# A linear-attention and snake-MLP kernel on one core: batch 0's loads, opening and three later orders rearranged

## Chip, core and metric

The kernel runs on one core of a Trainium2 chip. The metric is the device time of one execution in microseconds; the median of three runs before the change is 284.15 us (284.1 to 284.52). Times inside the kernel are from one profiled execution and are counted from its first instruction.

## What is computed

Inputs are float32: q, k, v of shape (8 batches, 8 heads, 576 rows, 64), w_in (512 x 2048), w_out (2048 x 512) and alpha (2048).

```python
q_s = softmax(q, axis=-1)                      # over the 64 of a head
k_s = softmax(k, axis=2)                       # over the 576 rows
kv  = einsum('bhsd,bhse->bhde', k_s, v)
x   = einsum('bhsd,bhde->bhse', q_s, kv)       # -> (4608 tokens, 512)
h   = x @ w_in
s   = sin(alpha * h)
g   = h + s * s / (alpha + 1e-9)
out = g @ w_out                                # (4608, 512)
```

## The kernel before

**Tiling.** A batch's 576 rows lie as 64 groups of J = 9 rows, and two heads share the 128 partitions; `ii` (0 or 1) names a half of the eight heads. The 4,608 tokens are worked in nine tiles of MF = 512 (index `t`), and the 2,048 columns of w_in in 16 blocks of 128 (index `ni`). A slot (`h_slot`) is four matmuls over `ki` (the four parts of the 512 inputs), a sine on ScalarE, a square on ScalarE, GpSimd or VectorE, and `combine` on VectorE (L270), which writes `g`. The output matmuls (L274) sum over the 16 blocks.

**Attention of a batch.** ScalarE takes the exponent of q and k (L119). q is normalised by its row sums (reduce L151, reciprocal L152, scale L153, into `qn`), then transposed into `qT`: batches 0 and 1 on TensorE, through PSUM (L203), the later ones by a DMA transpose on SyncE (L213). v is cast to bf16 into `vb`, with a column of ones beside each head. `kv_mm` (L174) multiplies the exponent of k with `vb`; the column of ones gives the sums of k, by which `kv_norm` (L184, L187) divides into `kbd`. `attn_chunk` and `attn_out` multiply `kbd` with `qT`; the result is cast into `xT`, the input of the slots.

**Order.** The schedule is written out by hand: each engine runs its instructions in the order of the program text, and a later one doesn't overtake an earlier one. `take(os, n)` issues the next n of the 64 output matmuls of a tile as work between other steps. A DMA is issued in its engine's order (SP is SyncE's queue, POOL is GpSimd's), and an instruction that waits on SP or POOL holds what stands behind it.

**Opening, up to the first slots.** SyncE loads batch 0: q's first half, k's first half, q's second, v's first, k's second (L299, called from the loop at L302). Of q only eight of the nine groups are loaded; the ninth of batches 0 and 1 comes later as `q8` (L474). GpSimd copies one element of k's first half into `held` (L332), which makes it wait for that load; behind it GpSimd issues v's second half in two parts, w_in in six column pieces (two DMAs each, one for either 64 partitions, L109) and w_out. w_in and w_out are cast from float32 to bf16 by the DMA. `warm_up(n)` (L343) issues n matmuls whose result nobody reads. Then exponents, norms, transposes and `kv_mm` follow for either half, the attention chunks, and the first matmuls of slots 0 to 3 over `ki` 0 and 1, which need only the first half of x.

**Batch 1** is loaded while tile 0's slots run: q by halves, then k and v by halves (L420, L428). Its attention stands between the output matmuls of tile 0: 46 of them, `transpose_q1(0)`, four, `kv_mm` of the first half, `kv_norm`, four, `x_half(0)`, `transpose_q1(1)`, two, `kv_mm` of the second half, `kv_norm`, five, `x_half(1)`, the rest. `x_half` and the transposes share two PSUM banks (pool "a").

**Batch 2** has its attention between the output matmuls of tile 1: four chunks (`c` from 0 to 3) with one output matmul behind each, then a piece for the last three groups. Its DMA transpose is issued in two halves; chunks 2 and 3 need the second.

**The loop over t from 3 on** does the slots of tile t, the output matmuls of tile t - 1 (an accumulator is copied out after every 16 and stored by two DMAs on SyncE, L286 and L289), and the attention of batch t + 1. `q_transpose_dma` of that batch and the loads of the one after it are issued at `ni == 4`; the attention's first matmul that needs the transpose comes at `ni == 9`.

Of the kernel before, what the change touches and what calls it, by code (L numbers as in the profile page):

```python
# [15 lines left out]
F32 = mybir.dt.float32  # L16
# [7 lines left out]
def kernel(  # L24
# [14 lines left out]
    nc = tc.nc  # L39
# [77 lines left out]
    def exp_to(dst, src, iis=range(2)):  # L117
        for ii in iis:
            nc.scalar.activation(dst[:, :, ii * 128:(ii + 1) * 128].rearrange("p j (x d) -> p x j d", x=2),  # L119
                                 src[:, ii::2], AX.Exp)  # L120
# [2 lines left out]
        A["qe", b] = att2.tile([128, J, 4 * D], BF16, name="qe")  # L123
        exp_to(A["qe", b], staged["q", b])

    def exp_half(name, b, ii, j1=J):
        if ii == 0:
            A[name + "e", b] = att2.tile([128, J, 4 * D], BF16, name=name + "e")
        exp_to(A[name + "e", b][:, 0:j1], staged[name, b][:, :, 0:j1], (ii,))

    def exp_k(b):
        A["ke", b] = att2.tile([128, J, 4 * D], BF16, name="ke")
# [165 lines left out]
    def load0(eng, n, t, ii, j0=0, j1=J):  # L298
        eng.dma_start(out=staged[n, 0][:, ii::2, j0:j1].rearrange("p i j d -> p i (j d)"),  # L299
                      in_=src_view(t, 0)[:, ii::2, j0 * D:j1 * D])  # L300

    for n, t, ii in (("q", q, 0), ("k", k, 0), ("q", q, 1), ("v", v, 0), ("k", k, 1)):  # L302
        load0(nc.sync, n, t, ii, 0, 8 if n == "q" else J)
    nc.scalar.dma_start(out=alpha_rows, in_=moe_alpha.rearrange("(no ni) -> no ni", ni=128))
    make_identity(nc, ident)
    DVE_CP(identb, ident)
# [23 lines left out]

    held = singles.tile([128, 1], F32, name="held")
    GP_CP(held, staged["k", 0][:, 0, 0, 0:1])  # L332
    load0(GP, "v", v, 1, 0, 5)
    load0(GP, "v", v, 1, 5, 9)
    for c0, c1 in ((0, 256), (256, 512), (512, 768), (768, 1024), (1024, 1536), (1536, 2048)):
        load_win(c0, c1)
    for c in range(2):
        load_wout(4 * c, 4 * c + 4)
# [1 line left out]
    def warm_up(n):  # L340

        for _ in range(n):
            nc.tensor.matmul(warm, identb, A["qe", 0][:, 0:4, 0:128], start=True, stop=True)  # L343

    exp_half("q", 0, 0, 8)
    exp_half("k", 0, 0)
    exp_half("q", 0, 1, 8)
    warm_up(7)  # L350
    norm_q(0, [V, V], 8)
    q_tile(0)
    q_transpose_ii(0, 0, 0, 8, tp0)
# [52 lines left out]
    def take(it, n=1000):  # L406
        for _ in range(n):
            if next(it, 0) == 0:
                return
# [4 lines left out]
    with ES:  # L414
        def load_q1(ii):
            if ii == 0:
                staged["q", 1] = stage.tile([128, 4, J, D], F32, name="st_q", tag="st")
            st = staged["q", 1]
            DVE_CP(st[:, ii, 0, 0:1], zero)
            nc.sync.dma_start(out=st[:, ii::2, 0:8].rearrange("p i j d -> p i (j d)"),  # L420
                              in_=src_view(q, 1)[:, ii::2, 0:8 * D])

        def load_kv1():
            for n in "kv":
                staged[n, 1] = stage.tile([128, 4, J, D], F32, name=f"st_{n}", tag="st")
# [12 lines left out]

        accs = [bank(kind) for kind in "bbll"]
        os = o_quad(0, accs, [DVE_CP, ACT_CP, DVE_CP, DVE_CP])  # L440
        take(os, 46)
        for ii in range(2):
            exp_half("q", 1, ii, 8)
        norm_q(1, [GP, V], 8)
        GP_CP(held, staged["k", 1][:, 0, 0, 0:1])
        load_wout(14, 16)

        def cast_v1(ii, eng):
            vv = vb[1].rearrange("p j (i c) -> p i j c", i=4)
            eng(vv[:, 2 * ii:2 * ii + 2, :, 0:D], staged["v", 1][:, ii::2])  # L450

        exp_half("k", 1, 0)
        cast_v1(0, ACT_CP)
        exp_half("k", 1, 1)
        def transpose_q1(ii):
            tp = ps_h[0].tile([128, 8, 128], BF16, name="tp", tag="a")
            q_transpose_ii(1, ii, 0, 8, tp)
            DVE_CP(q_tile(1)[:, ii, 0:8], tp)

        transpose_q1(0)  # L460
        take(os, 4)

        def x_half(ii):
            xp = [bank("a") for _ in range(2)]
            for e in range(2):
                attn_chunk(1, 2 * ii + e, 0, 8, xp[e])
            for e in range(2):
                (ACT_CP, DVE_CP)[e](xT[:, 2 * ii + e, MF:2 * MF], xp[e])
# [24 lines left out]
        load("v", v, 3)  # L493

        def late_q8(ni):
            if ni == 11:
                tp = ps_k.tile([128, 2, 2, 128], BF16, name="tp", tag="a")
                for b in range(2):
                    for ii in range(2):
                        nc.tensor.transpose(tp[:, ii, b], A["qe", 1][:, J - 2 + b, ii * 128:(ii + 1) * 128], identb)  # L500
                DVE_CP(A["qT", 1][:, :, J - 2:J], tp)
            elif ni == 15:
                xp = ps_k.tile([128, 4, 2, P], F32, name="xp", tag="a")
                for c in range(4):
# [75 lines left out]
    for t in range(3, nT):  # L580
        b = t + 1 if t + 1 < B else None
        os = o_stream(t - 1)
        done = 0
        if b is not None:

            exp_q(b)
            exp_k(b)
            cast_v(b, [GP_CP, GP_CP])
            norm_q(b, [GP])
            take(os, 8)  # L590
            done = 8
        for ni in range(nN):
            hp = mm_h(t, ni)
            if b is not None:
                if ni == 4:
                    q_transpose_dma(b)
                    if b + 1 < B:
                        load_batch(b + 1)
                attn_back(b, ni - 5)
            s = sine(t, ni, hp, "A")  # L600
            combine(t, ni, hp, s)
            want = 23 + 2 * (t == 3) + 21 * ni // 8 if b is not None else 4 * (ni + 1)
            take(os, min(64, want) - done)
            done = min(64, want)
        take(os)
# [36 lines left out]
```

## Time and profile before

| what | value |
|---|---|
| median of three runs | 284.15 us |
| the profiled execution, its own time | 284.61 us |
| its span, first to last instruction | 282.8 us |
| DVE / ACT / POOL busy | 189.1 / 225.2 / 83.6 us |
| granted TensorE clock | 1.000 |
| DMA packets | 39,127, 45.80 MB |
| output matmuls, L274, into `op` | 496, 124.1 us busy |
| slot matmuls, L254, into `hp` | 512, 128.3 us busy |

Busy times of matmuls overlap, since they are pipelined, so a busy PE isn't PE at its peak. In a row of the timeline the columns are start, duration, engine, line, operation, what it writes and reads, its shape and how many were merged; in square brackets stands the idle time of that engine before it and what ended it. PE is the matrix unit, PEld its weight load, DVE VectorE, ACT ScalarE, POOL GpSimd, SPq SyncE's queue.

### The profile page before, as it was taken

The numbers are of one execution on the slowest core, as the hardware profiler recorded it, in microseconds if no ns is written. First come the engines' busy times: TensorE is split into PE (matmuls) and PEld (weight loads), VectorE is DVE, ScalarE is ACT, GpSimd is POOL, SyncE is SP. The second block draws the span as 40 slices with busy tenths as digits, with TensorE's granted clock in tenths as the row PEclk, the third lists the DMA queues.
The fourth block names the chain that finished last, engine by engine and source line by source line (L and its number), as shares of the span: only waits on it lengthen the run. The fifth ranks groups of instructions, "written<-read, shape, count | busy, mean of one in ns | idle before, by whom it ended". The sixth has DMA issues, their size and how long they took to land.

```text
span 282.8 us, 4841 instructions
## 1 busy us (share of the span) xinstructions
PE 272.3 (96%) x1857; PEld 128.0 (45%) x1857; DVE 189.1 (67%) x286; ACT 225.2 (80%) x320; POOL 83.6 (30%) x80
## 2 busy tenths in 40 slices
PE   2999999999999999999999999999999999999994
PEld 1444444444444444444544444444444444444443
DVE  3968778899977768756875677667775555555412
ACT  4889667999489998899989998999877777777400
POOL 2989411777666550035012500241000000000000
PEclk9999999999999999999999999999999999999999
DMA  6999989996599018931991099019011111111143
GB/s 256 306 195 234 300 278 320 361 352 226 125 233 387 6 37 198 386 116 35 263 398 42 14 271 404 23 24 160 2 37 37 37 39 37 37 37 43 44 103 74
DMA packets 39127, 45.80 MB, mean 162 GB/s; under 512 B 17072, under 2 KB 22464, under 8 KB 39104
## 3 DMA queue, kind: packets, MB, share of 16 engines
q1 hardware_dynamic: 33360, 40.57, 47.0%
q0 software_dynamic: 5552, 4.79, 10.1%
q8 instruction: 14, 0.23, 0.3%
q10 hardware_dynamic: 192, 0.14, 0.2%
q14 instruction: 9, 0.07, 0.1%
HBM read 36.71 MB, written 9.44 MB: 163 GB/s over the span
## 4 chain that ended last, share of the span: by engine, by line
PE 82%; DMA 6%; ACT 5%; issue 2%; DVE 2%; POOL 1%; SPq 1%
PE hp L254 35%; PE op L274 32%; PE lp L274 2%; PE hp L274 2%; PE lp L254 2%; DMA qT<-qn 2%; ACT s L260 2%; DMA win<-in_moe_w_in_dram 2%; PE xp L223 2%; DMA st_k<-in_k_dram 2%; PE kvp L174 1%; PE op L612 1%; PE op L254 1%; PE kvp L254 1%; DVE qs L151 1%
## 5 line engine op out<-in xcount | busy, mean ns | idle before, releaser
L270 DVE SCALAR_TENSOR_TENSOR g<-s,inva_sb,hp 128x512 bf16<-128x512 f32 x128 | 94.3, 746 | 58.6 <-ACT s L262 52.9
L254 PE MATMUL hp<-xT,win 128*128 128x512 bf16 x512 | 128.3, 379 | 0.7 <-DMA win<-in_moe_w_in_dram 0.7
L274 PE MATMUL op<-wout,g 128*128 128x512 bf16 x496 | 124.1, 379 | 0.0
L260 ACT ACTIVATE s<-hp,alpha_sb 128x512 f32<-128x512 f32 x128 | 86.2, 682 | 24.3 <-PE hp L254 23.9
L254 PEld LDWEIGHTS <-win 128*128 128x128 bf16 x576 | 56.0, 98 | 67.9 <-DMA win<-in_moe_w_in_dram 0.8
L274 PEld LDWEIGHTS <-g 128*128 128x128 bf16 x560 | 53.9, 98 | 61.1 <-issue 0.4
L262 ACT ACTIVATE s<-s 128x512 f32<-128x512 f32 x112 | 70.5, 630 | 3.5
L264 POOL TENSOR_TENSOR s<-s 128x512 f32<-128x512 f32 x29 | 30.3, 1061 | 21.6 <-ACT s L260 21.6
L153 POOL TENSOR_TENSOR qn<-qe,qs 128x1152 bf16<-128x1152 bf16 (+1 forms) x12 | 25.1, 2110 | 33.0 <-DVE qs L147 24.3
L286 DVE COPY o<-op 128x512 f32<-128x512 f32 (+2 forms) x33 | 22.1, 670 | 9.9 <-PE op L274 7.6
L138 POOL CAST vb<-st_v 128x1152 bf16<-128x1152 f32 x12 | 14.7, 1257 | 46.9 <-DMA st_v<-in_v_dram 32.9
L119 ACT ACTIVATE qe<-st_q 128x1152 bf16<-128x1152 f32 (+1 forms) x16 | 17.5, 1130 | 5.0 <-DMA st_q<-in_q_dram 4.8
L119 ACT ACTIVATE ke<-st_k 128x1152 bf16<-128x1152 f32 x16 | 17.9, 1151 | 1.5 <-DMA st_k<-in_k_dram 1.5
L146 DVE TENSOR_REDUCE qs<-qe 128x36 f32<-128x2304 bf16 x5 | 12.8, 2553 | 7.9 <-ACT qe L119 7.9
L226 DVE CAST xT<-xp 128x512 bf16<-128x512 f32 (+1 forms) x18 | 13.5, 751 | 0.1
L151 DVE TENSOR_REDUCE qs<-qe 128x16 f32<-128x1024 bf16 (+1 forms) x6 | 7.5, 1252 | 3.8 <-ACT qe L119 3.8
L119 ACT ACT_TABLE_LOAD x7 | 9.0, 1283 | 1.3 <-PEq L626 1.2
L274 PE MATMUL lp<-wout,g 128*128 128x512 bf16 x32 | 9.1, 380 | 0.0
L274 PE MATMUL hp<-wout,g 128*128 128x512 bf16 x32 | 8.9, 380 | 0.0
L223 PE MATMUL xp<-qT,kbd 128*128 128x256 bf16 (+1 forms) x40 | 8.2, 286 | 0.3 <-DMA qT<-qn 0.3
L174 PEld LDWEIGHTS <-ke 64*64 64x64 bf16 x576 | 5.7, 108 | 4.7 <-ACT vb L329 1.3
L187 DVE TENSOR_TENSOR kbd<-kvp,kvr 64x256 bf16<-64x256 f32 (+1 forms) x20 | 7.4, 368 | 0.5
(83 smaller groups left out, 135.6 us busy)
## 6 DMA issues: line engine op xcount, KB each, us to landing
out_dram<-o SPq DMA_DIRECT2D x70, 128.0 KB, 2.4
st_q<-in_q_dram SPq DMA_DIRECT2D x6, 1152.0 KB, 6.3
st_k<-in_k_dram SPq DMA_DIRECT2D x6, 1152.0 KB, 8.8
st_v<-in_v_dram SPq DMA_DIRECT2D x6, 1152.0 KB, 11.1
st_k<-in_k_dram SPq DMA_DIRECT2D x4, 576.0 KB, 6.7
st_q<-in_q_dram SPq DMA_DIRECT2D x4, 512.0 KB, 5.2
st_v<-in_v_dram SPq DMA_DIRECT2D x3, 576.0 KB, 7.6
wout<-in_moe_w_out_dram POOLq DMA_DIRECT2D x3, 512.0 KB, 9.6
```

The costliest lines, as they stand in the source:

```text
L119: nc.scalar.activation(dst[:, :, ii * 128:(ii + 1) * 128].rearrange("p j (x d) -> p x j d", x=2), src[:, ii::2], AX.Exp)
L138: engs[ii](vv[:, 2 * ii:2 * ii + 2, :, 0:D], staged["v", b][:, ii::2])
L153: engs[ii % len(engs)].tensor_tensor(qn[:, ii, 0:j1].rearrange("p j (x d) -> p j x d", x=2), qe[:, ii], part.unsqueeze(3).to_broadcast([12 ...
L223: nc.tensor.matmul(xp[:, e, 0:n], kt[:, e, ii], qT[:, ii, j0:j1, e * 64:(e + 1) * 64], start=True, stop=True)
L226: eng(xT[:, 2 * ii:2 * ii + 2, c0:c0 + n], xp[:, :, 0:n])
L254: nc.tensor.matmul(hp, win[:, ki, ni * 128:(ni + 1) * 128], xT[:, ki, t * MF % NX:t * MF % NX + MF], start=(ki == 0), stop=(ki == 3))
L260: nc.scalar.activation(s, hp, AX.Sin, scale=alpha_sb[:, ni:ni + 1])
L262: nc.scalar.activation(s, s, AX.Square)
L264: nc.gpsimd.tensor_tensor(s, s, s, op=ALU.mult)
L270: nc.vector.scalar_tensor_tensor(G[t][:, ni], in0=s, scalar=inva_sb[:, ni:ni + 1], in1=hp, op0=ALU.mult, op1=ALU.add)
L274: nc.tensor.matmul(acc, G[t][:, ni, j * 128:(j + 1) * 128], wout[:, ni, :], start=(ni == 0), stop=(ni == nN - 1))
L286: eng(o[:, cols], acc)
```

## The change

Five things change. (1) SyncE loads batch 0 in another order: q's first half in two parts of four groups, q's second half, k, v, k, v, the last v half in two parts; GpSimd loads no v any more. (2) w_in's first 512 columns come as two halves of rows (`ki` 0 and 1, then 2 and 3) in place of two halves of columns; the other pieces stay. (3) The opening's exponents, sums, scales and casts are cut otherwise and shared anew between ScalarE and VectorE, and TensorE's transposes of q's second half stand behind the first two attention chunks; the warm-up matmuls are 7, 2 and 2 in place of 7, 2 and 3. (4) In batch 1, two output matmuls stand ahead of `transpose_q1(1)`, not behind it; in batch 2, three follow chunk 1 in place of one. (5) In the loop over t, the DMA transpose and the next batch's loads are issued at `ni == 3` in place of 4.

```diff
-    for n, t, ii in (("q", q, 0), ("k", k, 0), ("q", q, 1), ("v", v, 0), ("k", k, 1)):
-        load0(nc.sync, n, t, ii, 0, 8 if n == "q" else J)
+    for n, t, ii, j0, j1 in (("q", q, 0, 0, 4), ("q", q, 0, 4, 8), ("q", q, 1, 0, 8), ("k", k, 0, 0, J), ("v", v, 0, 0, J),
+                             ("k", k, 1, 0, J), ("v", v, 1, 0, 5), ("v", v, 1, 5, J)):
+        load0(nc.sync, n, t, ii, j0, j1)
...
     GP_CP(held, staged["k", 0][:, 0, 0, 0:1])
-    load0(GP, "v", v, 1, 0, 5)
-    load0(GP, "v", v, 1, 5, 9)
-    for c0, c1 in ((0, 256), (256, 512), (512, 768), (768, 1024), (1024, 1536), (1536, 2048)):
+    for k0 in (0, 2):
+        load_win(0, 512, k0, k0 + 2)
+    for c0, c1 in ((512, 768), (768, 1024), (1024, 1536), (1536, 2048)):
         load_win(c0, c1)
...
+    def sum_q0(ii, j0, j1):
+        nc.vector.tensor_reduce(qs0[:, j0:j1, 2 * ii:2 * ii + 2], ...)
+    def inv_q0(ii):
+        nc.vector.reciprocal(qs0[:, 0:8, 2 * ii:2 * ii + 2], qs0[:, 0:8, 2 * ii:2 * ii + 2])
+    def scale_q0(ii, j0, j1):
+        nc.vector.tensor_tensor(qn0[:, ii, j0:j1]..., qe0[:, j0:j1, ii * 128:(ii + 1) * 128]..., qs0..., op=ALU.mult)
...
-    exp_half("q", 0, 0, 8)
+    for j0 in (0, 4):
+        exp_half("q", 0, 0, j0 + 4, j0)
+        sum_q0(0, j0, j0 + 4)
+    warm_up(7)
+    inv_q0(0)
+    scale_q0(0, 0, 8)
+    exp_half("q", 0, 1, 8)
+    sum_q0(1, 0, 8)
     exp_half("k", 0, 0)
-    exp_half("q", 0, 1, 8)
-    warm_up(7)
-    norm_q(0, [V, V], 8)
+    inv_q0(1)
     q_tile(0)
     q_transpose_ii(0, 0, 0, 8, tp0)
-    cast_v0(0, 0, 9, ACT_CP)
+    warm_up(2)
+    cast_v0(0, 0, 5, DVE_CP)
+    cast_v0(0, 5, 9, ACT_CP)
     ACT_CP(A["qT", 0][:, 0, 0:8], tp0)
     exp_half("k", 0, 1)
+    kv_mm(0, 0, ps_k, split=True)
     warm_up(2)
-    kv_mm(0, 0, ps_k, split=True)
-    warm_up(3)
+    scale_q0(1, 0, 4)
     kv_norm(0, 0, 1)
-    tp1 = ps_l.tile([128, 8, 128], BF16, name="tp", tag="l")
-    q_transpose_ii(0, 1, 0, 8, tp1)
-    cast_v0(1, 0, 5, ACT_CP)
-    cast_v0(1, 5, 9, DVE_CP)
+    scale_q0(1, 4, 8)
+    cast_v0(1, 0, 5, DVE_CP)
+    cast_v0(1, 5, 9, ACT_CP)
     xp = [bank("b") for _ in range(2)]
     for c in range(2):
         attn_chunk(0, c, 0, 8, xp[c])
+    tp1 = ps_l.tile([128, 8, 128], BF16, name="tp", tag="l")
+    q_transpose_ii(0, 1, 0, 8, tp1)
...
         x_half(0)
+        take(os, 2)
         transpose_q1(1)
-        take(os, 2)
         kv_mm(1, 1, ps_k, split=True)
...
         (ACT_CP, DVE_CP)[c % 2](xT[:, c, c0:c0 + 6 * P], xp)
-        take(os, 1)
+        take(os, 3 if c == 1 else 1)
...
-                if ni == 4:
+                if ni == 3:
                     q_transpose_dma(b)
                     if b + 1 < B:
                         load_batch(b + 1)
```

More of the change, by code (lines that the diff above doesn't have):

```diff
@@ L124, in exp_q, with exp_half @@
         exp_to(A["qe", b], staged["q", b])
-    def exp_half(name, b, ii, j1=J):
-        if ii == 0:
+    def exp_half(name, b, ii, j1=J, j0=0):
+        if (name + "e", b) not in A:
             A[name + "e", b] = att2.tile([128, J, 4 * D], BF16, name=name + "e")
-        exp_to(A[name + "e", b][:, 0:j1], staged[name, b][:, :, 0:j1], (ii,))
+        exp_to(A[name + "e", b][:, j0:j1], staged[name, b][:, :, j0:j1], (ii,))
     def exp_k(b):
@@ L343, in warm_up @@
             nc.tensor.matmul(warm, identb, A["qe", 0][:, 0:4, 0:128], start=True, stop=True)
-    exp_half("q", 0, 0, 8)
+    qe0 = A["qe", 0] = att2.tile([128, J, 4 * D], BF16, name="qe")
+    qn0 = A["qn", 0] = att1.tile([128, 2, J, 2 * D], BF16, name="qn")
+    qs0 = small.tile([128, J, 4], F32, name="qs")
+    def sum_q0(ii, j0, j1):
+        nc.vector.tensor_reduce(qs0[:, j0:j1, 2 * ii:2 * ii + 2],
+                                qe0[:, j0:j1, ii * 128:(ii + 1) * 128].rearrange("p j (x d) -> p j x d", x=2),
+                                axis=AXL.X, op=ALU.add)
+    def inv_q0(ii):
+        nc.vector.reciprocal(qs0[:, 0:8, 2 * ii:2 * ii + 2], qs0[:, 0:8, 2 * ii:2 * ii + 2])
+    def scale_q0(ii, j0, j1):
+        nc.vector.tensor_tensor(qn0[:, ii, j0:j1].rearrange("p j (x d) -> p j x d", x=2),
+                                qe0[:, j0:j1, ii * 128:(ii + 1) * 128].rearrange("p j (x d) -> p j x d", x=2),
+                                qs0[:, j0:j1, 2 * ii:2 * ii + 2].unsqueeze(3).to_broadcast([128, j1 - j0, 2, D]), op=ALU.mult)
+    for j0 in (0, 4):
[6 more added lines that the diff above has]
+    sum_q0(1, 0, 8)
     exp_half("k", 0, 0)
-    exp_half("q", 0, 1, 8)
-    warm_up(7)
-    norm_q(0, [V, V], 8)
+    inv_q0(1)
     q_tile(0)
     q_transpose_ii(0, 0, 0, 8, tp0)
-    cast_v0(0, 0, 9, ACT_CP)
+    warm_up(2)
+    cast_v0(0, 0, 5, DVE_CP)
+    cast_v0(0, 5, 9, ACT_CP)
     ACT_CP(A["qT", 0][:, 0, 0:8], tp0)
     exp_half("k", 0, 1)
+    kv_mm(0, 0, ps_k, split=True)
     warm_up(2)
-    kv_mm(0, 0, ps_k, split=True)
-    warm_up(3)
+    scale_q0(1, 0, 4)
     kv_norm(0, 0, 1)
-    tp1 = ps_l.tile([128, 8, 128], BF16, name="tp", tag="l")
-    q_transpose_ii(0, 1, 0, 8, tp1)
-    cast_v0(1, 0, 5, ACT_CP)
-    cast_v0(1, 5, 9, DVE_CP)
+    scale_q0(1, 4, 8)
+    cast_v0(1, 0, 5, DVE_CP)
+    cast_v0(1, 5, 9, ACT_CP)
     xp = [bank("b") for _ in range(2)]
```

## Prediction

> **What bounds the kernel now.** I read the page first, then the sums by stretch, then the timeline around every place where the next matmul starts later than the one before it allows. The page:
>
> ```profile
> PE 272.3 (96%) x1857; PEld 128.0 (45%) x1857; DVE 189.1 (67%) x286; ACT 225.2 (80%) x320; POOL 83.6 (30%) x80
> ```
>
> TensorE is the bound, and almost all of its idle time is at the start. Matmuls of 512 columns follow each other every 0.216 us (eight of them take 1.73 us in the chain that ended last). Held against that step, PE from 16.4 us on has only three pauses over 0.2 us, and the change has an edit at each. The opening:
>
> ```profile
> 5.99 0.19 POOL L332 COPY held<-st_k 128x1 f32<-128x1 f32 x1 [4.68 <-DMA st_k<-in_k_dram]
> 6.11 1.63 POOL L299 DMA_DIRECT2D st_v<-in_v_dram  x2
> 7.73 4.96 POOL L109 DMA_DIRECT2D win<-in_moe_w_in_dram  x8
> 13.75 1.02 PE L254 MATMUL hp<-xT,win 128*128 128x512 bf16 x4 [0.67 <-DMA win<-in_moe_w_in_dram]
> ```
>
> Here the reader sees that the first useful matmul (13.75) waits for w_in, which POOL may issue only when k's first half has landed. But an earlier start is worth something only if the data of batch 1 comes earlier too. The sums by stretch (PE, PEld, DVE, ACT, POOL busy, clock, DMA share, GB/s):
>
> ```profile
> 17.00:26.00 9.00, 9.00 (x43) 4.11 (x42) 7.42 (x12) 8.85 (x16) 7.46 (x9) 1.00 1.23 202
> 26.00:33.00 7.00, 7.00 (x35) 3.14 (x33) 6.17 (x10) 5.88 (x9) 3.59 (x4) 1.00 1.19 261
> 33.00:39.00 6.00, 6.00 (x35) 2.97 (x34) 3.41 (x6) 3.04 (x3) 2.86 (x3) 1.00 1.05 402
> 41.00:44.00 3.00, 2.54 (x52) 1.39 (x52) 2.60 (x7) 0.87 (x2) 0.00 (x0) 1.00 0.58 107
> ```
>
> The DMA share is at or above 1 until 39 us (the loads that cast count their smaller written bytes, hence 202 GB/s). So when batch 1's v lands is settled by bytes, not by when PE asks. The timeline there:
>
> ```profile
> 38.18 1.17 ACT L450 CAST vb<-st_v 128x1152 bf16<-128x1152 f32 x1 [0.88 <-DMA st_v<-in_v_dram]
> ...
> 41.48 0.77 DVE L450 CAST vb<-st_v 128x1152 bf16<-128x1152 f32 x1 [0.33 <-DMA st_v<-in_v_dram]
> 42.02 0.61 PE L203 MATMUL tp<-identb,qn 128*128 128x128 bf16 x8 [0.46 <-ACT xT L468]
> 42.28 0.69 DVE L468 CAST xT<-hp 128x512 bf16<-128x512 f32 x1
> 42.89 0.68 DVE L458 COPY qT<-tp 128x1024 bf16<-128x1024 bf16 x1
> 43.54 0.17 DVE L184 RECIPROCAL kvr<-kvp 128x2 f32<-128x2 f32 x1
> 43.74 0.59 DVE L187 TENSOR_TENSOR kbd<-kvp,kvr 64x128 bf16<-64x128 f32 x2
> ```
>
> VectorE runs from v's landing (41.46) to 44.33 without a gap, and the matmul pair of x_half(1), which reads kbd, starts at 44.50. Only 0.1 us of slack is left after a semaphore's 0.05. The two later pauses:
>
> ```profile
> 72.70 0.38 PE L274 MATMUL op<-wout,g 128*128 128x512 bf16 x1
> 73.15 0.32 PE L231 MATMUL hp<-qT,kbd 128*128 128x384 bf16 x1
> ...
> 110.31 1.03 PE L254 MATMUL hp<-xT,win 128*128 128x512 bf16 x4
> 111.63 0.39 PE L223 MATMUL xp<-qT,kbd 128*128 128x256 bf16 x2 [0.30 <-DMA qT<-qn]
> ```
>
> 73.15 - 72.70 - 0.216 is 0.23 us; 111.63 - 110.31 - 4 x 0.216 is 0.46 us.
>
> **The change, part by part.**
>
> *Opening, loads.* The bytes up to w_in's first 512 KB are the same, in another order on SP: q, q, k, v, k, v. From landings of before (issue plus time to landing: 4.51 for q, then +1.43 for k, +1.27 q, +1.42 v, +1.48 k) I get q complete at 5.8, k's first half at 7.2, v 8.65, k 10.1, and v's second half at 11.55, since 576 KB on SP took 1.42 to 1.48 and on POOL 1.54 (10.11 to 11.65). POOL's held copy moves from 5.99 to 7.25, and with it w_in's first issue from 7.73 to 7.4: it no longer stands behind v's two issues (0.90 and 0.73 us). Three SP issues more cost 0.5 us each of SP's queue, which next has work at 23.43.
>
> Runs get shorter: q's halves and v's parts have 1,024 to 1,280 bytes where the loads of before have 2,048 and 2,304. The trace has packets of 256 bytes (q8's load) at 18 ns, of 2,048 at 84 and of 2,304 at 93: a fixed 8.6 ns and 0.0366 per byte, so 46 and 55.5 for the new ones. Over 16 engines q's first half costs 512 x 46 / 16 - 256 x 84 / 16 = 0.13 us more and v's second 256 x (46 + 55.5) / 16 - 256 x 93 / 16 = 0.14: I take 0.25. From the one side it is nothing (as by the 2,048-byte row); from the other, q8's load as a whole (256 KB in about 1.8 us) in place of its packets makes the same line give 0.63. Against it, w_in's first 512 columns come in runs twice as long: a 256 KB piece landed every 0.68 us when 256 wide and every 0.64 when 512 wide (1.28 for twice the bytes), so 4 x 0.04 is 0.15 back. Net: batch 1's data 0.10 us later; bounds -0.3 (short runs free, the later narrow pieces faster too) and +0.5.
>
> *Opening, compute.* Durations from the rows: exp of 1,024 takes 1.06, reduce and scale 1.22, reciprocal 0.25, ACT cast 0.73 for 640, DVE cast 0.43 for 512. ACT: q in two of 0.6 (to 5.15), q 6.9, k 8.4, v's part 9.3, qT copy 10.3, k 11.45, v's part 12.2, xT 12.8, qT 13.8 (14.20 before). DVE: two sums 5.8, reciprocal 6.1, scale 7.35, sum 8.6, reciprocal 8.85, cast 9.4, scale 10.05, kv_norm 10.95, scale 11.6, cast 12.1, xT 12.8, kv_norm 13.65. So x's first half is ready at 12.8 and w_in's first row pair (all four output blocks) at 13.5: 13.61 less two pieces' gain. PE: four matmuls to 14.4, the attention pair to 14.85, DVE's two xT casts 14.65 to 16.05. Slot 0's last part resumes at 16.1, was 16.37: the opening gains 0.3 us. One warm-up fewer overall (12 to 11) lies in idle PE. From both sides: +0.9 if w_in is there at 12.85, -0.35 if w_in's packets start 2.4 us after issue (as w_out's did at 36.41 beside running loads) and take 30% of the engines from v.
>
> *Batch 1.* The transposes waited 0.6 us for a bank (ACT's cast, 41.39 to 41.97). Two output matmuls moved ahead of them fill 0.43. PE would reach x_half(1) at 44.50 - 0.3 - 0.43 = 43.77, but kbd comes from v's landing: 41.46 + 0.10 + 2.87 + 0.05 = 44.48. So opening and filler together pay 0.02 us, and PE waits the rest. The same cap hides an opening up to 0.35 worse.
>
> *Batch 2, c == 1.* Two more output matmuls (0.43) before the third chunk, which waits for its transpose's landing: 0.23 gained. What is late next: that chunk's casts, by 0.2; DVE is in its 2.55 us reduce until 73.7 and casts at 74.73 anyway.
>
> *ni 3 for 4, in the loop.* SP's order at t=3 is the point:
>
> ```profile
> 102.68 4.82 SPq L289 DMA_DIRECT2D out_dram<-o  x4
> 107.60 1.87 SPq L213 DMA_TRANSPOSE qT<-qn  x1
> ```
>
> Its input is ready at 103.85 (POOL's two qn end there), but the transpose stands behind the second output pair, whose DVE copy starts at 105.69. Moved past it, it issues at 103.9, lands 4 us later at 107.9, and is needed at 111.17: 0.46 gained. The output pair then waits behind the transpose and three loads until 107.5, 1.1 us later; o has four buffers and the next copy is at 113.4. For t=4 to 6 no queue order changes and PE had no wait there: nothing.
>
> Sum: 0.02 + 0.23 + 0.46 = 0.71 us. The profiled execution took 284.61 (282.8 of span and 1.8 around it), 0.46 above the median of the runs; I take the difference as the same: span 282.1, execution 283.9, median 284.15 - 0.71 = **283.4**.
>
> The chip's notes speak against the order of loads: the Trainium skill, DMA: Bandwidth & Descriptors, Queues, rings and completion order, says that each engine takes turns between queues, a packet at a time, and its Latency section puts the first byte of a POOL-issued load at about 1 us. By that w_in would share with k and v from 8.4 us. Before, v's 320 KB on POOL's queue were issued at 6.11 and landed at 10.88, 0.77 after k on SP (10.11): behind it, not beside it. By the rule the sum would be that of the slower rival.
>
> **Rivals.** (1) *The opening pays too.* If batch 1's v lands 0.6 us earlier, 0.3 + 0.43 come through: 0.73 + 0.69 = 1.42, 282.7. For it: w_in's narrow pieces are the slowest loads. Against: equal bytes, a DMA share of 1. (2) *The short runs cost more*, the 0.63 of the far side, and batch 1's v is 0.48 us late: 41.46 + 0.48 + 2.92 = 44.86 against 44.50 gives back 0.36, leaving 0.33: 283.8, no difference that can be told. For it: 202 GB/s in the stretch of narrow pieces. Against: q's and k's loads, of unlike runs, moved at one rate. I count 0.2% (0.57 us) as what a measurement of this kernel can tell. (3) *Slower: w_in takes half of the engines from k and v.* Place: 8.5 us on (issue 7.4 plus 1.1, SP's own lag at the start, 0.74 to 1.87). SP's loads have 2.7 us left, become 5.4, v's last part lands at 14.35; ACT casts it (15.0), then xT (15.6) and qT (16.6); the attention pair starts at 16.65 instead of 14.61: 2.04 lost. The filler returns 0.43, the later edits 0.69: +0.92, 285.1. It decides from a loss of 1.7 in the opening on, so from sharing before about 8.8. For it: 26 to 33 us, where a q load took 6.1 us to land beside w_out. Against: the row of v's load above. (4) *The transposes don't move*, because POOL ends later than 107: 0.46 missing, 283.9; POOL's row ends at 103.85, so I fold it into (2).
>
> **How the numbers follow.** Forecast 50%, its own range 283.1 to 283.7; (1) 13%; (2) with (4) 22%; (3) 15%. Of the forecast's half 5% lie within 0.2%: faster 0.45 + 0.13 = 0.58, same 0.27, slower 0.15. The range 282.8 to 284.2 leaves out about 8% of (1)'s side and 12% of (3)'s.
>
> **What would show it.** Right: kbd of batch 1 still released by v's landing near 41.5, x_half(1) near 44.4 with a PE pause of 0.3 to 0.6 ahead of it; no pause near 73 nor 111; SP's transpose at t=3 near 103. Wrong: v of batch 1 landing before 41 or after 42; v of batch 0 landing after 13; PE at half rate (0.427 us per matmul, as at 5.64 to 8.15 us) after 13.5, which would cost 0.21 per matmul.

## The result, and the profile after

The change made the kernel slower: a median of 286.25 us (285.49 to 288.83) beside 284.45 us for the kernel before in the same comparison, a ratio of 1.0063 with a 95% interval of 1.0047 to 1.0079. The forecast was 283.4 us, faster. The profiled execution took 286.75 us, with a span of 285.0 us (282.8 before).

The page of the changed kernel first, its busy times and the granted clock in 40 slices (7.1 us each):

```profile
PE 271.3 (95%) x1827; PEld 128.6 (45%) x1856; DVE 189.8 (67%) x289; ACT 224.9 (79%) x321; POOL 82.2 (29%) x78
...
PEclk9779999999999999999999999999999999999999
```

TensorE's work is the same, 271.3 us for 272.3, so the 2.2 us of span are waiting. The clock, 9 in every slice before, is lower in the second and third: the trouble lies in the first 20 us. The timeline there (start, duration, engine, line, in brackets the idle time and what ended it):

```profile
3.65 1.36 ACT L119 ACTIVATE qe<-st_q 128x512 bf16<-128x512 f32 x2 [1.14 <-DMA st_q<-in_q_dram]
8.55 1.06 ACT L119 ACTIVATE qe<-st_q 128x1024 bf16<-128x1024 f32 x1 [3.54 <-DMA st_q<-in_q_dram]
9.98 0.19 POOL L333 COPY held<-st_k 128x1 f32<-128x1 f32 x1 [8.68 <-DMA st_k<-in_k_dram]
10.11 7.08 POOL L109 DMA_DIRECT2D win<-in_moe_w_in_dram  x11
11.94 0.71 PE L174 MATMUL kvp<-vb,ke 64*64 64x65 bf16 x36 [3.50 <-DVE vb L330]
16.01 1.46 PE L254 MATMUL hp<-xT,win 128*128 128x512 bf16 x3
```

q's first half comes early, in two parts at 3.63 and 4.36 us, as meant. But ScalarE then waits 3.54 us for q's second half, which lands at 8.53, 4.17 us after the load before it; the working had 5.8. Everything behind it in SyncE's queue is late by as much: k 9.93, v 11.36, k 12.86, v's last part 14.58 (11.65 before, 11.55 in the working). `held`, w_in's first issue (10.11 for 7.4) and the first slot matmul (16.01; 13.75 before) follow.

The sums by stretch tell whether the engines had nothing to do or were slow. The columns are the busy times of PE, PEld, DVE, ACT and POOL, the clock, the DMA share and GB/s. The clock's 1.00 can't be relied on in these rows: in the kernel before, PE's warm-ups from 5.64 us on are 0.43 us apart, twice the step at full rate. Before:

```profile
3.00:4.50 1.50, 0.25 (x1) 0.28 (x2) 0.43 (x2) 0.00 (x0) 0.00 (x0) 1.00 1.05 407
4.50:6.00 1.50, 0.36 (x1) 0.11 (x1) 0.38 (x1) 1.10 (x2) 0.01 (x1) 1.00 1.04 406
6.00:7.50 1.50, 1.50 (x5) 0.59 (x4) 1.43 (x3) 1.39 (x2) 1.50 (x3) 1.00 1.06 415
7.50:9.00 1.50, 1.50 (x8) 0.67 (x6) 1.50 (x2) 1.14 (x2) 1.50 (x4) 1.00 1.04 410
```

and after:

```profile
3.00:4.50 1.50, 0.29 (x2) 0.21 (x3) 0.62 (x3) 0.75 (x2) 0.00 (x0) 1.00 0.99 236
4.50:6.00 1.50, 1.50 (x5) 0.47 (x4) 1.42 (x3) 0.51 (x1) 0.00 (x0) 1.00 0.88 267
6.00:7.50 1.50, 1.50 (x6) 0.47 (x5) 1.24 (x2) 0.00 (x0) 0.00 (x0) 1.00 1.02 338
7.50:9.00 1.50, 0.94 (x10) 0.44 (x8) 0.00 (x0) 0.45 (x1) 0.00 (x0) 1.00 0.95 317
```

The DMA engines are as busy (share 0.88 to 1.02) but move 236 to 338 GB/s where they moved 406 to 415. That is 720 KB less in 6 us, or 1.8 us at 410 GB/s. Single packets say the same: 41 of them took over 250 ns (up to 1,076) between 3.5 and 8.4 us, and none before; 84 ns is usual for a 2,048-byte one.

How it reaches the end is seen in batch 1 (timeline of the changed kernel):

```profile
44.16 0.75 DVE L476 CAST vb<-st_v 128x1152 bf16<-128x1152 f32 x1
45.12 0.61 PE L203 MATMUL tp<-identb,qn 128*128 128x128 bf16 x8
46.57 0.59 DVE L187 TENSOR_TENSOR kbd<-kvp,kvr 64x128 bf16<-64x128 f32 x2
47.21 0.60 PE L231 MATMUL hp<-qT,kbd 128*128 128x512 bf16 x2
```

The same matmuls, `x_half(1)`, in the kernel before:

```profile
44.50 0.59 PE L231 MATMUL hp<-qT,kbd 128*128 128x512 bf16 x2
```

Batch 1's last v lands at 44.07, 2.61 us later than before (41.46). `x_half(1)` starts 3.14 us behind it (3.04 before). From its start to the end of the span it is 285.0 - 47.21 = 237.79 us; before it was 282.8 - 44.50 = 238.30. So the later edits gave 0.51 us in these two executions, and the opening took 47.21 - 44.50 = 2.71.

Two ways lead to `x_half(1)`, and here they ended close together. The one that ended last was PE's own work: from 18.14 to 47.20 us PE is busy for 28.64 of 29.06 us, without a pause over 0.16. It came late for two reasons. Its first slot was 2.26 us late (16.01 for 13.75). And from there to `x_half(1)` it took 31.20 us, where the profiles of e13, e16 and e17 below, at full clock and as free of pauses, all took 30.37; for 1.70 us of it (16.01 to 17.71) the clock stood at half. PE was busy for 1.48 us of these, half of which, 0.7 us, is my estimate of what the clock cost there, and it waited 0.22 us for w_in. The other way is v's landing: the shortest step from v to `x_half(1)` in any profile is 2.86 us, so v would have let it start at 44.07 + 2.86 = 46.93. The two are 0.28 us apart, and both are late by the opening.

The later places look as the prediction wanted them. Batch 2's third chunk, and SyncE's queue with its cause at t = 3:

```profile
74.98 0.38 PE L274 MATMUL op<-wout,g 128*128 128x512 bf16 x1
75.20 0.33 PE L231 MATMUL hp<-qT,kbd 128*128 128x384 bf16 x1
...
102.13 4.21 POOL L153 TENSOR_TENSOR qn<-qe,qs 128x1152 bf16<-128x1152 bf16 x2 [3.33 <-issue]
105.17 1.12 SPq L289 DMA_DIRECT2D out_dram<-o  x2
106.39 2.26 SPq L213 DMA_TRANSPOSE qT<-qn  x1
112.80 1.03 PE L254 MATMUL hp<-xT,win 128*128 128x512 bf16 x4
113.66 0.38 PE L223 MATMUL xp<-qT,kbd 128*128 128x256 bf16 x2
```

75.20 - 74.98 is 0.22 us, one matmul's step, so the pause of 0.23 is gone. The transpose is issued at 106.39, as soon as POOL's two `qn` end (106.34), and the matmul that needs it starts at 113.66 = 112.80 + 4 x 0.216, without a wait.

### The profile page after: what moved, and what is told of

It is laid out like the page before. It is cut to its first block, busy times and chain, and to the rows that moved or that the text cites. A ratio compares the mean times of both kernels' runs of the same rounds, so it can differ in the third digit from the quotient of the medians.

```text
span 285.0 us, 4816 instructions
## 1 busy us (share of the span) xinstructions
PE 271.3 (95%) x1827; PEld 128.6 (45%) x1856; DVE 189.8 (67%) x289; ACT 224.9 (79%) x321; POOL 82.2 (29%) x78
## 4 chain that ended last, share of the span: by engine, by line
PE 91%; DMA 5%; issue 1%; POOL 1%; DVE 1%; SPq 0%
PE hp L254 38%; PE op L274 37%; DMA st_k<-in_k_dram 3%; PE lp L274 2%; PE lp L254 2%; PE hp L274 2%; DMA win<-in_moe_w_in_dram 2%; PE kvp L174 2%; PE xp L223 2%; PE op L638 1%; PE op L254 1%; PE kvp L254 1%; POOL win L109 1%; PE hp L231 1%; SPq L299 0%
## 5 line engine op out<-in xcount | busy, mean ns | idle before, releaser
L274 PE MATMUL op<-wout,g 128*128 128x512 bf16 x477 | 121.6, 379 | 1.4 <-issue 0.6
L119 ACT ACTIVATE qe<-st_q 128x1152 bf16<-128x1152 f32 (+2 forms) x17 | 17.7, 1075 | 8.2 <-DMA st_q<-in_q_dram 8.0
L226 DVE CAST xT<-xp 128x512 bf16<-128x512 f32 (+1 forms) x18 | 13.5, 750 | 0.0
L174 PE MATMUL kvp<-vb,ke 64*64 64x65 bf16 x576 | 7.2, 200 | 3.5 <-DVE vb L330 3.5
L109 POOL DMA_DIRECT2D win<-in_moe_w_in_dram x12 | 7.5, 641 | 0.9 <-DMA win<-in_moe_w_in_dram 0.7
```

The lines of the kernel that those rows point to most:

```text
L174: nc.tensor.matmul(kvp[64 * x:64 * x + 64, e, ii * 65:(ii + 1) * 65], ke[r, j, h * 64:(h + 1) * 64], vt[r, j, h * 65:(h + 1) * 65], start= ...
L274: nc.tensor.matmul(acc, G[t][:, ni, j * 128:(j + 1) * 128], wout[:, ni, :], start=(ni == 0), stop=(ni == nN - 1))
```

## The experiments

Four theories stood at the start. A: what costs is a load of q behind another load of q. B: the split of q's first half costs, by its runs of 1,024 bytes (B1) or because two small loads of 256 KB stand at the head of the queue (B2). C: the slow load is chance. And the later edits, or the clock, might carry part of the loss. Medians are given with that of the kernel before in the same comparison in brackets, and ratios with their 95% interval. A "landing" is the last event of a load in the trace; v(1) is the landing of batch 1's last v.

**e1: the changed kernel once more**, unchanged.

> The changed kernel once more, for a second profile. In the first, q's second half landed at 8.53 us in place of the 5.8 that I had worked out, 4.2 us after the first half, and the TensorE clock stood at one half from 10.9 to 17.7 us. Theory A (q's second half is slow because it directly follows the first half of the same tensor) and theory B (the runs of 1,024 bytes slow the queue) expect it again: landing at 8 to 9 us, time 1.5 to 2 us above before. Theory C (a chance disturbance of that one execution) expects a landing near 5.8 here, and a time that differs from run to run.

286.02 us (285.21), 1.004 [1.0005, 1.0075]. q's second half lands at 7.78, 3.34 us after the load before it, v(1) at 43.27. The size varies between executions, the slow load doesn't go away: C falls.

**e2: the kernel before with the later edits alone.**

```diff
-        transpose_q1(1)
         take(os, 2)
+        transpose_q1(1)
...
-        take(os, 1)
+        take(os, 3 if c == 1 else 1)
...
-                if ni == 4:
+                if ni == 3:
```

> The kernel before with only the three later edits: two output matmuls ahead of batch 1's second transposes, three behind batch 2's chunk 1, the loop's transposes and loads at ni 3. My sum says 0.02 + 0.23 + 0.46 = 0.7 us faster than before (283.7 if before is at 284.45). All of the loss then lies in the opening. If the later edits lose time themselves, it is not faster.

284.07 us (285.21), 0.9964 [0.9947, 0.9981]: 1.1 us gained. All of the loss is in the opening.

**e3: the changed kernel with q's first half whole.**

```diff
-    for n, t, ii, j0, j1 in (("q", q, 0, 0, 4), ("q", q, 0, 4, 8), ("q", q, 1, 0, 8), ...
+    for n, t, ii, j0, j1 in (("q", q, 0, 0, 8), ("q", q, 1, 0, 8), ...
```

> The changed kernel, but q's first half comes as one load with runs of 2,048 bytes, as before; q's second half still directly behind it. Theory B expects the slow load to vanish: q's second half lands near 5.8, and the time falls by about 2 us, to 0.5 below before. Theory A expects it to stay: landing at 8 to 9, time as the changed kernel's or 0.3 above it, because the exponent of q's first half starts later.

284.5 us (285.21), 0.9976 [0.9957, 0.9996]. Its timeline:

```profile
4.99 1.15 ACT L119 ACTIVATE qe<-st_q 128x512 bf16<-128x512 f32 x2 [2.48 <-DMA st_q<-in_q_dram]
6.32 1.06 ACT L119 ACTIVATE qe<-st_q 128x1024 bf16<-128x1024 f32 x1 [0.18 <-DMA st_q<-in_q_dram]
```

Landings 4.96 and 6.30: the second q load comes 1.34 us behind the first, though it is q behind q. A falls; the split is what costs.

**e4: k between the two halves of q**, the split kept.

```diff
-    ... ("q", q, 0, 4, 8), ("q", q, 1, 0, 8), ("k", k, 0, 0, J), ...
+    ... ("q", q, 0, 4, 8), ("k", k, 0, 0, J), ("q", q, 1, 0, 8), ...
```

> The changed kernel with the loads in the order q, q, k, q, v, k, v, v: k's first half stands between q's halves as it did before. Theory A expects the slow load to vanish: k lands near 6.0, q's second half near 7.3, the time falls by about 2 us, to 0.5 below before. Theory B expects slow packets to stay, now in k's load: k lands at 7.5 or later, the time as the changed kernel's.

288.24 us (285.21), 1.0094 [1.0067, 1.0122]. Now k is the slow one: it lands at 7.50, q behind it at 8.75. Whatever load stands third is hit.

**e5: q's first half still in two loads of 256 KB, but by heads, with runs of 2,048 bytes.**

```diff
-    ... ("q", q, 0, 0, 4), ("q", q, 0, 4, 8), ("q", q, 1, 0, 8), ...
+    for i in (0, 2):
+        nc.sync.dma_start(out=staged["q", 0][:, i:i + 1, 0:8]..., in_=src_view(q, 0)[:, i:i + 1, 0:8 * D])
+    ... ("q", q, 1, 0, 8), ...
```

> The changed kernel with q's first half still in two loads of 256 KB, but cut between heads, so that the runs keep 2,048 bytes. Theory B1 (short runs at the head of the queue slow the loads behind them) expects q's second half near 6.0 to 6.5 us and a time 0.3 to 1.0 us below before. Theory B2 (it is the number of small loads ahead, not their runs) expects the slow loads again: q's second half at 7.5 or later and 1 to 2 us above before.

285.54 us (285.05), 1.0023 [0.9995, 1.005]. Landings 3.48, 4.17 and 7.58: the third load takes 3.41 us with long runs too. B1 falls, B2 holds. Its timeline shows a side effect:

```profile
4.24 1.28 ACT L119 ACT_TABLE_LOAD   x1 [4.24 <-DMA st_q<-in_q_dram]
5.54 1.15 ACT L119 ACTIVATE qe<-st_q 128x512 bf16<-128x512 f32 x2
```

Here the exponent's table load stands behind the wait for q, not ahead of it, and the early q gains nothing.

**e6: the kernel before with nothing but that split.**

```diff
-    for n, t, ii in (("q", q, 0), ("k", k, 0), ("q", q, 1), ("v", v, 0), ("k", k, 1)):
+    load0(nc.sync, "q", q, 0, 0, 4)
+    load0(nc.sync, "q", q, 0, 4, 8)
+    for n, t, ii in (("k", k, 0), ("q", q, 1), ("v", v, 0), ("k", k, 1)):
```

> The kernel before with one edit: q's first half comes in the two group parts of the change (runs of 1,024 bytes), nothing else is touched. B1 and B2 both expect k's first half, the load behind it, at 7 to 7.5 us in place of 5.94, and the time 1 to 2 us above before, since every later load moves with it. If the loss needs the change's other parts (the new order, the shared casts, the clock), the time is that of before within 0.5 us.

288.43 us (285.05), 1.0121 [1.0083, 1.016]; k at 7.75 (5.94 before), v(1) at 43.80:

```profile
7.77 1.16 ACT L119 ACTIVATE ke<-st_k 128x1152 bf16<-128x1152 f32 x1 [0.93 <-DMA st_k<-in_k_dram]
```

One line of the change, alone, is enough to make the kernel before as slow. (Part of it is the table load again: the exponent of q starts at 5.78 instead of 4.5.)

**e7: the changed kernel with 18 warm-ups for the first `warm_up(2)`**, so that PE isn't idle from 8.4 to 11.9 us and the clock stays.

```diff
-    warm_up(2)
+    warm_up(18)
```

> The changed kernel with 18 warm-up matmuls in place of 2 behind the first transposes, which fill about 3.5 us of the 3.7 that TensorE stood idle there. If part of the loss is the clock (half rate from 10.9 to 17.7 us in the first profile), the mean granted clock comes back to 0.997 or more, and the time falls by 0.6 to 1.2 us against the changed kernel, still above before by about 0.5 to 1. If the late loads are all of it, the clock rises but the time stays within 0.3 of the changed kernel's.

285.84 us (285.05), 1.003 [1.001, 1.005]. The clock is back to 0.997 to 1.0 in all executions. By the ratios the time is 0.3 us better than e1's and 0.9 better than in the first comparison, and the intervals overlap with both. The sums by stretch, of the changed kernel and then of e7:

```profile
12.00:15.00 3.00, 3.00 (x46) 1.55 (x46) 2.68 (x7) 2.44 (x4) 3.00 (x6) 0.50 1.05 192
15.00:18.00 3.00, 2.78 (x46) 1.52 (x45) 1.32 (x4) 2.97 (x5) 2.06 (x5) 0.55 1.11 143
```

```profile
12.00:15.00 3.00, 2.62 (x48) 1.07 (x47) 1.36 (x5) 2.25 (x3) 2.92 (x6) 1.00 1.08 199
15.00:18.00 3.00, 2.54 (x51) 1.53 (x51) 2.35 (x7) 2.85 (x4) 1.65 (x3) 1.00 1.20 148
```

The half clock is real, and it slows PE, but little of the loss is its own: at full clock PE waits for the late loads instead (0.86 us in e7, up to 43.24, for the cast of batch 1's first v), and v(1) lands at 44.85. In the changed kernel's profile, with v's landing as it was, only the 0.28 us between the two ways could be won back. In its 22 executions the two at clock 1.0 took 286.65 and 286.79 us, more than the median; the five at 0.993 or less took 286.75 to 288.83, but they don't say whether the clock or late data came first.

**e8: q whole, and k's first half split instead** (256 and 320 KB, third and fourth in the queue).

```diff
-    ... ("q", q, 0, 0, 4), ("q", q, 0, 4, 8), ("q", q, 1, 0, 8), ("k", k, 0, 0, J), ...
+    ... ("q", q, 0, 0, 8), ("q", q, 1, 0, 8), ("k", k, 0, 0, 4), ("k", k, 0, 4, J), ...
```

> The changed kernel with q's first half whole (2,048-byte runs), but k's first half in two parts of four and five groups (runs of 1,024 and 1,280 bytes). B1 in the form that only the head of the queue matters expects v's first half near 9.1 us and a time as with whole q, 0.5 below before. Theory B3 (short runs anywhere in the opening slow what follows) expects v's first half at 10.5 or later, and a time 1 us or more above whole q.

285.02 us (285.05), 1.0002 [0.9971, 1.0033]. Landings 4.96, 6.29, 6.96, 8.03, 9.47: no slow load. Small loads later in the queue do no harm.

**e9: the changed kernel with the second small load issued on ScalarE's queue.**

```diff
-    ... ("q", q, 0, 0, 4), ("q", q, 0, 4, 8), ("q", q, 1, 0, 8), ...
+    ... ("q", q, 0, 0, 4), ("q", q, 1, 0, 8), ...
+    load0(nc.scalar, "q", q, 0, 4, 8)
```

> The changed kernel, but the second of q's two small loads is issued on ScalarE's queue at the same time as the first on SyncE's, so that q's second half is SyncE's second load and issued 0.5 us earlier. If the slow load is slow because the engines reach the third load of one queue sooner after its issue (1.8 us) than in the kernel before (3.6 us), the earlier issue brings q's second half to 6.5 us or before and the time to within 0.5 us of before. If two small loads at the head are enough, whatever queue they stand on, it lands at 7.5 or later again and the time is 1 us or more above before.

284.96 us (285.11), 0.9998 [0.9978, 1.0018]. Its timeline and its sums by stretch:

```profile
4.22 1.15 ACT L119 ACTIVATE qe<-st_q 128x512 bf16<-128x512 f32 x2 [1.14 <-DMA st_q<-in_q_dram]
5.87 1.06 ACT L119 ACTIVATE qe<-st_q 128x1024 bf16<-128x1024 f32 x1 [0.51 <-DMA st_q<-in_q_dram]
```

```profile
3.00:4.50 1.50, 0.00 (x0) 0.00 (x0) 0.00 (x0) 0.36 (x2) 0.00 (x0) 1.00 1.10 390
4.50:6.00 1.50, 0.63 (x2) 0.31 (x3) 0.58 (x3) 0.99 (x3) 0.00 (x0) 1.00 1.05 410
```

The same bytes in the same small pieces, and 390 to 410 GB/s: q complete at 5.85, k 7.25, v 8.69, k 10.17, v 11.71. So the load behind two small ones is not slow when one of them is on another queue. e9 doesn't part the queue from the time of issue, the other reading that its expectation names: q's second half was also issued 0.5 us earlier (1.26 for 1.77 us). By the first packets, the slow loads of the change, e1, e4, e6 and e7 began 1.7 to 1.9 us after their issue and e9's 2.6 us after it. In e10, next, a load that began 1.4 us after issue was fast (k) and one that began 2.8 us after it was slow (q's second half), which speaks against that reading without settling it. (v(1) was still 42.88 here: two w_in pieces landed 2.4 us apart, at 14.41 and 16.78, which the runs below don't all show.)

**e10: one small load, k, the other small one, then q's second half.**

```diff
-    ... ("q", q, 0, 0, 4), ("q", q, 0, 4, 8), ("q", q, 1, 0, 8), ("k", k, 0, 0, J), ...
+    ... ("q", q, 0, 0, 4), ("k", k, 0, 0, J), ("q", q, 0, 4, 8), ("q", q, 1, 0, 8), ...
```

> The changed kernel with one small load at the head: q (4 groups), k's first half, q (4 groups), q's second half, v, k, v, v. If any load behind a small first one is slow, k lands at 6 us or later in place of about 5.1, and the time is 1 to 2 us above before. If it takes two small ones at the head, k lands near 5.1, q's parts at 5.8 and 7.2, and the time is 0.5 below before or up to 0.5 above it (q's first half is complete 1.4 us later).

290.54 us (285.11), 1.0201 [1.018, 1.0222], the slowest of all. k at 5.17 and the second small load at 5.83 come at nearly the usual rate (k 1.50 us behind the load ahead): one small load at the head does next to no harm. Much of the loss is another mechanism, rival (3)'s:

```profile
5.22 0.19 POOL L333 COPY held<-st_k 128x1 f32<-128x1 f32 x1 [3.91 <-DMA st_k<-in_k_dram]
5.34 5.04 POOL L109 DMA_DIRECT2D win<-in_moe_w_in_dram  x8
8.07 1.06 ACT L119 ACTIVATE qe<-st_q 128x1024 bf16<-128x1024 f32 x1 [1.59 <-DMA st_q<-in_q_dram]
13.19 1.16 ACT L119 ACTIVATE ke<-st_k 128x1152 bf16<-128x1152 f32 x1 [1.59 <-DMA st_k<-in_k_dram]
```

`held` waits for k, so w_in is issued from 5.34 and moves beside batch 0's loads: k's second half lands at 13.17, v's last part at 17.06, v(1) at 48.83. q's second half, at 8.05, was slow too (2.2 us). That wasn't w_in's doing: the first packet of GpSimd's queue ran at 9.37 us. So the load behind the second small one was slow here as well, by some 0.9 us, with k between the two.

**e11: e2 with w_in's first pieces by row halves.**

```diff
-    for c0, c1 in ((0, 256), (256, 512), (512, 768), (768, 1024), (1024, 1536), (1536, 2048)):
+    for k0 in (0, 2):
+        load_win(0, 512, k0, k0 + 2)
+    for c0, c1 in ((512, 768), (768, 1024), (1024, 1536), (1536, 2048)):
```

> The kernel before with the three later edits and w_in's first 512 columns by row halves; loads and opening as before. My price for the row halves was 4 x 0.04 = 0.15 us less load time: 0.1 to 0.3 faster than the later edits alone (0.9964 of before). If the row halves cost something (the first slots wait for other rows), it is 0.2 or more slower than these.

284.42 us (285.11), 0.9989 [0.9958, 1.002]; v(1) at 43.25. No gain over e2 (0.9964) is to be seen.

**e12: e2 with w_out's last piece held until k's second half of batch 1 has landed**, to free engines for v.

```diff
-        GP_CP(held, staged["k", 1][:, 0, 0, 0:1])
+        GP_CP(held, staged["k", 1][:, 1, 0, 0:1])
```

> The kernel before with the three later edits, and the last w_out load, which shares the engines with batch 1's last v load, held until k's second half has landed rather than its first. In the runs so far the span is batch 1's last v landing plus 240.6 to 241.0 us, in all kernels with the later edits. If that landing sets the time, v lands 0.4 to 0.6 us earlier (near 41.0) and the time falls by 0.2 to 0.6 against the later edits alone. If not, or if w_out now comes too late for the output matmuls that need it (before 44), the time is the same or up to 1 us longer.

285.76 us (285.11), 1.0034 [1.0011, 1.0057], a miss: v(1) is 41.70, no earlier than e2's 41.53, and w_out, landing at 44.49, makes PE wait 0.98 us, up to 44.53.

**e13, e14, e15: the mended openings, one piece taken back each.** e13 is e9 with w_in's column pieces of before; e14 is e9 with v's second half on GpSimd's queue as before; e15 is e3 with the column pieces.

```diff
 e13 (from e9), e15 (from e3)
-    for k0 in (0, 2):
-        load_win(0, 512, k0, k0 + 2)
-    for c0, c1 in ((512, 768), (768, 1024), (1024, 1536), (1536, 2048)):
+    for c0, c1 in ((0, 256), (256, 512), (512, 768), (768, 1024), (1024, 1536), (1536, 2048)):
 e14 (from e9)
-    ... ("k", k, 1, 0, J), ("v", v, 1, 0, 5), ("v", v, 1, 5, J)):
+    ... ("k", k, 1, 0, J)):
...
+    load0(GP, "v", v, 1, 0, 5)
+    load0(GP, "v", v, 1, 5, J)
```

> The changed kernel with the second small q load on ScalarE's queue (no slow load) and w_in by column pieces as before. If the row halves are the second part of the loss, it is 0.5 to 1.0 us faster than the same kernel with row halves (0.9998 of before), near the later edits alone: 0.9965 to 0.9985 of before. If they cost nothing, it stays at 0.9990 to 1.0005.

> The changed kernel with the second small q load on ScalarE's queue, row halves kept, but v's second half back on GpSimd's queue ahead of w_in, as before. If the move of v to SyncE's queue is the second part of the loss, 0.5 to 1.0 us faster than 0.9998 of before. If it is neutral, as my sum had it within 0.1 us, 0.9990 to 1.0005.

> The changed kernel with q's first half as one load and w_in by column pieces. With row halves it stood at 0.9976 of before. If the row halves cost 0.5 us or more, it reaches 0.9945 to 0.9960, at or below the later edits alone (0.9964), since its opening starts the slots no later. If they cost nothing, it stays at 0.9970 to 0.9985.

e13: 283.63 us (284.93), 0.9945 [0.9918, 0.9971], v(1) at 40.73. e14: 285.79 us, 1.0026 [0.9995, 1.0056], v(1) at 44.27. e15: 284.6 us, 0.9984 [0.9964, 1.0004]. So v's second half on SyncE's queue is no part of the loss. e13 looked like the best version, and like a price of the row halves; both needed a repeat.

**e16, e17, e18: e13, e9 and e2 again, together.**

> The changed kernel with its two small q loads on two queues and w_in by columns, again, on one chip with the two below. If it is the better version, 0.993 to 0.997 of before and below the later edits alone; if its first result (0.9945) was chance, 0.997 to 1.000.

> The same with w_in's first columns by row halves, the change's form. If the row halves cost, 0.3% or more above the column form of this call; if they don't, within 0.2% of it.

> The kernel before with the three later edits alone, again: 0.995 to 0.998 of before (0.9964 the first time; my sum said 0.9975).

e16: 283.83 us (284.30), 0.9976 [0.9962, 0.9991]. e17: 283.99 us, 0.9985 [0.9968, 1.0002]. e18: 283.43 us, 0.9965 [0.9948, 0.9981]. e16 misses the 0.993 to 0.997 that its expectation asked of the better version. Columns and rows differ by 0.16 us with overlapping intervals: no price of the row halves is shown, nor a gain. The best version that repeats is the kernel before with the later edits alone (0.9964 and 0.9965); its medians are below those of both kernels. Its `x_half(1)`, from its timeline:

```profile
41.32 0.76 DVE L450 CAST vb<-st_v 128x1152 bf16<-128x1152 f32 x1
43.51 0.59 DVE L187 TENSOR_TENSOR kbd<-kvp,kvr 64x128 bf16<-64x128 f32 x2
44.16 0.61 PE L231 MATMUL hp<-qT,kbd 128*128 128x512 bf16 x2
```

**Profiles side by side.** What is left of the span after v(1), and after the start of `x_half(1)`, in us:

| kernel | v(1) | `x_half(1)` | span | span - v(1) | span - `x_half(1)` |
|---|---|---|---|---|---|
| before | 41.46 | 44.50 | 282.81 | 241.3 | 238.3 |
| e13, mended opening | 40.73 | 44.27 | 281.98 | 241.3 | 237.7 |
| e18, later edits alone | 41.29 | 44.16 | 281.69 | 240.4 | 237.5 |
| e16, mended opening | 41.47 | 44.46 | 282.15 | 240.7 | 237.7 |
| e2, later edits alone | 41.53 | 44.97 | 282.52 | 241.0 | 237.6 |
| e12, w_out held | 41.70 | 45.61 | 283.23 | 241.5 | 237.6 |
| e3, q whole | 42.11 | 44.98 | 282.72 | 240.6 | 237.7 |
| e1, the change again | 43.27 | 46.13 | 283.85 | 240.6 | 237.7 |
| the change | 44.07 | 47.21 | 284.96 | 240.9 | 237.8 |
| e10 | 48.83 | 51.70 | 289.38 | 240.5 | 237.7 |

From `x_half(1)` to the end, all 18 profiles with the later edits took 237.5 to 237.8 us, and the two without them (before, e6) 238.3 and 238.5: all the rest is settled ahead of `x_half(1)`. v(1) goes with it closely, 2.9 to 3.1 us ahead, in 17 of the 20 profiles. In e2, e12 and e13 the step is 3.4 to 3.9 us: there PE's own work, in e12 with its wait for w_out, ended later than v's landing allowed.

## Why the prediction was wrong, step by step

**Opening, loads: the step that failed.** It priced the shorter runs at 0.25 us with bounds of 0 and 0.63 and gave q complete at 5.8. The trace has 8.53, and 7.78 in e1. The cost isn't in the runs (e5, 3.41 us with runs of 2,048 bytes) but in having two 256 KB loads ahead of the third at the head of one queue: the third takes 3.0 to 4.2 us instead of 1.3 to 1.45 whichever load it is (e4, e6), and the usual time when the first is whole (e3) or the second is on another queue (e9). The price of a packet was right: those of 1,024 and 1,280 bytes in the changed kernel's later loads took 46 and 55 ns, as worked out. Both bounds came from the time of packets in loads that had run at full rate; no row of before had small loads at the head of a queue, so the working bounded a size and left out a mechanism. Why the hardware does it is open: the runs show where it happens, not what in the DMA engines is short.

The rest of that step was right once the slow load was gone. e9 landed at 5.85, 7.25, 8.69, 10.17 and 11.71, against 5.8, 7.2, 8.65, 10.1 and 11.55 worked out.

The 0.15 us back for w_in's longer runs was not seen (e11 beside e2; e17 beside e16). Whether they cost anything is open too.

**Opening, compute.** Never tested as foreseen in the changed kernel, since the data were late. In e9, with loads on time, the first slot matmul started at 13.85 for 13.5, where w_in's landing ended its wait; in e16 and e17 at 14.09 and 13.80, where VectorE's cast of x did. e18, with the old opening, had it at 13.16. So the 0.3 us that the new opening was given didn't show. One reason is a side effect of the two queues: alpha, now behind q on ScalarE's queue, landed at 5.16 us in e16 (3.15 in the kernel before), its copy stands ahead in VectorE's order, and the first sum of q began at 5.97 us. What the opening would give with alpha on time is open.

**Batch 1: the cap is there, but it isn't the only one.** The working had the matmul 2.92 us behind v's landing; it was 3.14 in the change and 2.87 in e18. It was read as a shield ("hides an opening up to 0.35 worse"). But PE's own work is a second way to `x_half(1)`, and in the change both carried the late opening in full: 2.6 us of late v, 2.7 us lost at `x_half(1)`. Of the 2.6 us, 1.8 are the bytes missing from 3 to 9 us by the sums above; the rest I didn't take apart. The pause of PE that the working left ahead of `x_half(1)` isn't there in e13, e16 and e17 either: with no pause over 0.16 us PE comes to it at 44.27, 44.46 and 44.17, for 43.77 in the working, mainly because its first slot came at 13.8 to 14.1 and not at 13.5.

**Batch 2 and ni 3: right.** Both pauses are gone, by the rows shown. From `x_half(1)` to the end the change gained 0.51 us and e18 0.77 (238.30 - 237.53), for 0.69 worked out. By medians e2 and e18 gained 1.1 and 0.9 us, to which the repeatability of v's landing adds.

**The rivals.** (2) had the right place and sign, loads that cost more, but with packet lengths as the mechanism and 0.63 us as its end. (3), w_in sharing the engines with k and v, is a real mechanism: e10 shows it, when w_in is issued at 5.34. In the change w_in was issued at 10.11, because its gate was late as well. The row that the prediction held against (3) was misread: v's load on GpSimd's queue ran its first packet at 9.39 us, beside the last 0.7 us of k's load and not behind it. What (3) had wrong is when sharing starts: the first packet came 3.3 us after the issue there, 4.0 in e10 and 1.9 in the change, not 1.1. (1), with its early v, didn't come about in the change; in e13 v(1) was 0.73 us earlier than in the kernel before and `x_half(1)` only 0.23, since the opening wasn't earlier. (4) neither, the transposes moved as said.

**The signs named in advance** all showed: batch 1's v after 42, batch 0's v after 13, and PE at half rate after 13.5. PE, waiting for data, was idle from 8.43 to 11.94 us, and the clock stood at half from 10.88 to 17.71. The Trainium skill, TensorE: Matmul & The Clock Gate, HAM oscillation — how this bites in real kernels, says that idle gaps of more than about 3.4 us bring the clock down, and counts half of the time at half speed as lost. Here the clock was down 2.45 us into the gap, and in e1 a gap of 2.29 us was followed by 3.4 us at half clock, so the gap need not be that long. Half of 6.83 us would be 3.4 us lost, an estimate by that page; with v's landing as it was, the two ways to `x_half(1)` leave 0.28 us of it in the time.

## What to carry to other kernels

Cutting the first load so that work may start sooner can slow the whole queue behind it: look at the landing of the next loads and at GB/s beside the DMA share, not at the first landing alone. If the first load must be cut, put its pieces on two queues, and look what the second queue then delivers later. And where an engine's own work and a later transfer lead to the same point, find when each would get there: making one of them earlier earns only the distance to the other, and what holds up both costs its full delay.

## What the runs showed of the hardware

- Two 256 KB loads at the head of SyncE's queue make the third load take 3.0 to 4.2 us instead of 1.3 to 1.45, in the change with the DMA engines busy (share 0.88 to 1.02) at 236 to 338 GB/s. The same split third and fourth in the queue (e8), a single small load at the head (e10's first two landings behind it) or two queues (e9) don't show it; behind the second small load of e10 the next took 2.2 us. The Trainium skill, DMA: Bandwidth & Descriptors, Rules for kernel authors, says that spreading loads over issuing engines doesn't help bandwidth and only saves issue time. Here it brought 390 GB/s for 236 from 3.0 to 4.5 us, which is no more than whole loads have on one queue (e3, 401).
- ScalarE's first table load (1.28 us) stands nowhere in the program text. In e5 and e6, whose first exponent needs both small loads of q, it stood behind the wait for them, and that exponent began at 5.54 and 5.78 us, 1.37 us after its data landed; in the other 18 profiles it started at 1.2 to 1.8 us, ahead of the wait.
- GpSimd's queue shares the engines with SyncE's loads from its first packet on, and this came late: v's at 9.39 us in the kernel before (issued at 6.11), w_in's at 9.37 in e10 (issued at 5.34). In the kernel before, SyncE had 0.7 us of k left then, and v landed close behind it; in e10 three loads, and k landed at 13.17, v at 17.06.
